# Values of the full layers by halves of the heads, and a last normalisation tile by tile: a four-layer attention kernel

## The chip, the cores and the metric

The kernel runs on one core of a Trainium2 chip. Its time is that of one execution on the device, in microseconds (us). TensorE is called PE here, VectorE DVE, ScalarE ACT, GpSimd POOL and SyncE SP; SP issues the DMAs.

## What is computed

Four layers on x of 2048 rows (the sequence) by 512 columns. Each is a layer norm, an attention of 32 heads of 16 and a residual. Layers 0 and 2 share weights and look back over a window of 256 positions ("sliding"); layers 1 and 3 share other weights and attend to everything, with no mask ("full").

```python
def _A_ref(x, wqkv, wo):          # _B_ref: the same without the mask
    B, S, D = x.shape
    H = 32; Dh = D // H; W = 256
    qkv = (x @ wqkv).reshape(B, S, 3, H, Dh).transpose(2, 0, 3, 1, 4)
    q, k, v = qkv[0], qkv[1], qkv[2]
    scores = jnp.einsum("bhqd,bhkd->bhqk", q, k) * (Dh ** -0.5)
    idx = jnp.arange(S)
    mask = (idx[:, None] - idx[None, :] >= 0) & (idx[:, None] - idx[None, :] < W)
    p = _softmax(jnp.where(mask[None, None], scores, -1e9), axis=-1)
    o = jnp.einsum("bhqk,bhkd->bhqd", p, v)
    return o.transpose(0, 2, 1, 3).reshape(B, S, D) @ wo

x = x + _A_ref(_layernorm(x), A_wqkv, A_wo)
x = x + _B_ref(_layernorm(x), B_wqkv, B_wo)
x = x + _A_ref(_layernorm(x), A_wqkv, A_wo)
x = x + _B_ref(_layernorm(x), B_wqkv, B_wo)
```

Everything is float32.

## The kernel before

**Units.** The sequence is cut into 4 chunks of 512 queries (c = 0 to 3) and 16 key tiles of 128; the heads into 8 quads (qd = 0 to 7). A float32 product of a projection is made of float16 high and low parts, three products for each of four slices of 128 inputs: 12 matmuls give one output tile of 128 by 512. That is a *piece* of side work, and four pieces are a *work*: the keys K(l,c), queries Q(l,c), values VV(l,c) or output projection OO(l,c) of layer l and chunk c, 48 matmuls each. In layer 3 keys, queries and output projection are cut further by pairs of quads (K3, Q3, O3).

**Attention.** `attention` (L897) walks through chunks and quads (in layer 3 through pairs t, then chunks, then quads). In a full layer a quad has 16 steps, one for each key tile. A step makes two score tiles (`exps`, L655; matmuls L663), ACT takes the exp of each, 128 by 1024 (L667), and 8 matmuls two steps later multiply them with the values (L707). A column of ones in the values (17 columns per head) yields the sum. Three score buffers hold what PE is ahead of ACT. In a sliding layer a quad has three steps with narrower tiles; POOL masks their edges (L729, L732), and the matmuls with the values are at L739. `epilogue` (L626) divides, splits the result into high and low parts (L645, L646), and four DMAs put it into the transposed output tile `oh`. In full layers the low part (L646) is made on POOL.

**Side work.** The order of PE's instructions is written out by the program; the other engines' order comes from the framework's scheduler. Between the steps of attention the class `Side` (L808) emits pieces of works. In sliding layers a chunk has 24 steps, and `step` emits up to a piece or so per step by a planner's clock (a matmul costs .222 on it). In full layers `share` (L869) deals out single groups of matmuls against a budget; there a 128-wide product is cut into four matmuls of 32 columns (L407 to L409) that together fill the one free bank, `acc[1]` (`bank`, L389). The next tile waits until DVE has copied this bank. When the steps of a `Side` are over, `finish` (L880) forces out in one run whatever is left. A work may start when its dependencies are done and one of two weight buffers (`weights`, L372) is free.

**Values.** `values` (L567) multiplies the transposed chunk with the value weights, tile by tile (i = 0 to 3), and copies each into `vt`. In full layers a chunk's `vt` has 4 tiles by 32 heads by 17, in 4 buffers (tag "vf"), and all four chunks are made before the full layer starts: as side work of the sliding layer, in its tail, and the last one (`lasts`) in the very end. Order of the lists: side0 (L1039), side2 (L1048), side1 (L1057), side3 (L1063); tails and lasts (L1075 to L1077).

**The end of a sliding layer** is not beside any attention. `wo` (L591) makes the last chunk's residual: for each of four row tiles 12 matmuls, DVE multiplies and adds (L601, L602), x is stored, and `stats` (L429) takes mean and variance. After the fourth tile `norm` (L431) runs one `rsqrt` (L39, 12 small DVE operations on a column per tile) and then, per tile, three operations (L439 to L442) that write the normalised tile as high and low parts `xh`. `transpose` (L456) then issues four transposing DMAs on SP, which fill the chunk's `xc`. The chunk's keys follow: 4 pieces, each with a maximum over squares (L515, L530), a high and a low part (`sp`, L490 to L493) and DMAs into `kf` in DRAM; then `key_shift` (L555) sets a row of `kf` from these maxima. Only then can `load_full` (L684) load the first keys `kt` of the full layer. Meanwhile PE makes the values of the last chunk.

**The kernel's end** is the last epilogue and `wo_part` (L609) of the last pair and chunk: four tiles of 3 matmuls, on DVE a multiplication (L621) and an addition (L622) each, and a store.

Of the kernel before, what the change touches and what calls it, by code (L numbers as in the profile page):

```python
# [38 lines left out]
def rsqrt(nc, vp, tag, var):  # L39

    v = vp.tile([P, 4], F32, name=f"v{tag}", tag="lnv")
    y = vp.tile([P, 4], F32, name=f"y{tag}", tag="lny")
    z = vp.tile([P, 4], F32, name=f"z{tag}", tag="lnz")
# [145 lines left out]
def fast_path(ctx, tc, flag, a_x, a_wqkv, a_wo, b_wqkv, b_wo, out):  # L189
# [182 lines left out]
    def weights(ty, s, n, t=None):  # L372

        w = wp.tile([P, NC, 2, D], F16, name=f"w{n}", tag="w", bufs=WB)
        if t is None:
            nc.sync.dma_start(w, wd[ty, s])
            return w
        nc.sync.dma_start(w[:, :, :, :P], wd[ty, s][:, :, :, t * P:(t + 1) * P])
        return w
# [18 lines left out]
    def mms(ps, pairs, after=1.6):  # L398
# [6 lines left out]
        for i, (a, b) in enumerate(pairs):  # L405
# [6 lines left out]
            spent(MM)  # L412
            if i < len(pairs) - 1:
                if PH["full"]:
                    yield MM
            else:
                PH["free"] = clock[0] + after
# [13 lines left out]
    def norm(l, c, xs):  # L431

        mv = ST.pop((l, c))[1]
        y = rsqrt(nc, vp, f"{l}_{c}", mv[:, :, 1])
        out = []
        for i in range(4):
            xn = vp.tile([P, D], F32, name=f"xn{l}_{c}_{i}", tag="xn", bufs=1)
            xh = vp.tile([P, 2, D], F16, name=f"xh{l}_{c}_{i}", tag="xh", bufs=XNB)
            norm1 = lambda o: nc.vector.tensor_scalar(o, xs[i], mv[:, i, 0:1], y[:, i:i + 1], op0=ALU.subtract, op1=ALU.mult)  # L439
# [15 lines left out]

    def transpose(l, c, xns):  # L456

        xc = XC[l, c] = wp.tile([P, 2, NC, QC], F16, name=f"xc{l}_{c}", tag="xc", bufs=NQ)
        for i in range(4):
            yield "wait", XNR[l, c] + 2.3 * i  # L460
            nc.sync.dma_start(xc[:, :, :, i * P:(i + 1) * P].rearrange("p b k n -> p (b k) n"),
                              xns[i].rearrange("p b n -> p (b n)"), transpose=True)

    def project(l, s, c, act, ht=None, first=None):
# [3 lines left out]
        if not first:  # L468
            w = weights(ty, s, n, ht)
# [97 lines left out]
    def values(l, c, act, first=None):  # L567
        n = f"{l}_{c}"
        if not first:
            w = weights(l % 2, 2, f"v{n}")  # L570
            yield wait(8)
            xc = XC[l, c]
        vt = V[l, c] = wp.tile([P, 4, H, DH + 1], F32, name=f"vt{n}",
                               tag="vf" if l % 2 else "vw", bufs=NQ if l % 2 else VB)
        nc.gpsimd.memset(vt[:, :, :, DH:], 1.0)
        for i in range(4):
            ps = bank()
# [5 lines left out]
            if first:  # L583
                nc.vector.tensor_tensor(vt[:, i, :, :DH], src, first[2].rearrange("p (h d) -> p h d", d=DH), ALU.mult)
            elif act:
                nc.scalar.activation(vt[:, i, :, :DH], src, AF.Copy)  # L586
            else:
                nc.vector.tensor_copy(vt[:, i, :, :DH], src)
            yield -MM if PH["full"] else -12 * MM

    def wo(l, c):  # L591
# [4 lines left out]
        for i in range(4):  # L596
# [8 lines left out]
            if i == 3:  # L605
# [3 lines left out]
    def wo_part(c, t):  # L609
# [6 lines left out]
        for i in range(4):  # L616
            ps = bank()
            yield from mms(ps, [(o[:, a, i * P:(i + 1) * P], w[:, b, :]) for a, b in TERMS])
            d = vp.tile([P, D], F32, name=f"dx3_{c}_{t}_{i}", tag="xn", bufs=1)
            k = 4 * c + i  # L620
            nc.vector.tensor_tensor(d, ps, gcol[1], ALU.mult)  # L621
            nc.vector.tensor_add(xs[i], xs[i], d)  # L622
# [3 lines left out]
    def epilogue(l, c, qd, a):  # L626
# [19 lines left out]
        (nc.gpsimd if l % 2 else nc.vector).tensor_tensor(hl[:, 1], o, hl[:, 0], ALU.subtract)  # L646
# [52 lines left out]
    def attn_full(l, c, qd, kt, qt, a):  # L699
        for j in range(NT):  # L700
# [4 lines left out]
            def pv(j=j, es_=es_):  # L705
                for h in range(4):
                    nc.tensor.matmul(a[32 * h:32 * h + DH + 1, :], V[l, j // 4][:, j % 4, 4 * qd + h, :],  # L707
# [189 lines left out]
    def attention(l, works):  # L897
# [5 lines left out]
        for t in range(NHT if l == 3 else 1):  # L903
            for c in range(NQ):
                qds = range(2 * t, 2 * t + 2) if l == 3 else range(NQD)
                if l == 1:

                    sd = sd or Side(NT * NQD * NQ, works[0], works[1])
# [6 lines left out]
                for qd in qds:  # L915
                    nxt = load(l, c, qd + 1) if qd + 1 in qds else None
# [19 lines left out]
    def T(l, c):  # L936
        return Work(later(lambda: transpose(l, c, XN.pop((l, c)))), 0.0, ("T", l, c), [("N", l, c)], aside=True)
# [188 lines left out]
```

## Time and profile before

| | us |
|---|---|
| median of 3 runs | 2864.93 (2863.16 to 2867.7) |
| the profiled execution | 2864.46 |
| its span | 2862.7 |
| layer 0, chunk 1 of the attention | about 170 to 310 |
| end of layer 0 (no attention) | about 517 to 580 |
| layer 1, exps | 580.7 to 1526.9 |
| layer 2, attention | 1536 to 1836 |
| end of layer 2 (no attention) | 1836 to 1896 |
| layer 3, exps | 1896.1 to 2838.5 |

Busy shares of the whole span: PE 93%, ACT 82%, DVE 37%, POOL 22%. The mean granted clock of PE is 0.979.

How to read the profile: times are us from the span's start. A row of the timeline has the start, the length from the first to the last end of a group of equal instructions that follow each other, engine, line and operation, the tile written and those read, the shape, and the count; in brackets the idle time of the engine just before and what ended it. Matmuls are pipelined, so a group's length includes the last one's drain. A row of windows has the length of a stretch and the time that each engine was busy in it. A row of waits has the us in total, the times and the longest one.

### The profile page before, as it was taken

The numbers are of one execution on the slowest core, as the hardware profiler recorded it, in microseconds if no ns is written. First come the engines' busy times: TensorE is split into PE (matmuls) and PEld (weight loads), VectorE is DVE, ScalarE is ACT, GpSimd is POOL, SyncE is SP. The second block draws the span as 40 slices with busy tenths as digits, with TensorE's granted clock in tenths as the row PEclk, the third lists the DMA queues.
The fourth block names the chain that finished last, engine by engine and source line by source line (L and its number), as shares of the span: only waits on it lengthen the run. The fifth ranks groups of instructions, "written<-read, shape, count | busy, mean of one in ns | idle before, by whom it ended". The sixth has DMA issues, their size and how long they took to land.

```text
span 2862.7 us, 58733 instructions
## 1 busy us (share of the span) xinstructions
PE 2668.1 (93%) x23298; PEld 766.6 (27%) x23298; DVE 1048.1 (37%) x2194; ACT 2352.5 (82%) x2643; POOL 627.5 (22%) x1183
## 2 busy tenths in 40 slices
PE   8777989799999999999999888999999999999997
PEld 4222433322222222222223333322222222222221
DVE  7667656411113212311224667722222322223222
ACT  3443656299999999999996666569999999999996
POOL 3547565101100000000003567500000000000000
PEclk9888999899999999999999999999999999999998
DMA  6857666522223222322343665542433333333331
GB/s 225 229 181 191 219 189 201 179 101 88 88 70 104 90 70 88 111 83 70 97 112 116 177 189 146 161 135 89 126 102 103 113 121 119 111 101 110 112 97 57
DMA packets 317423, 363.10 MB, mean 127 GB/s; under 512 B 120913, under 2 KB 223825, under 8 KB 309841
## 3 DMA queue, kind: packets, MB, share of 16 engines
q1 hardware_dynamic: 317136, 359.24, 41.5%
q8 instruction: 185, 3.03, 0.4%
q14 instruction: 102, 0.83, 0.1%
HBM read 229.64 MB, written 96.99 MB: 114 GB/s over the span
## 4 chain that ended last, share of the span: by engine, by line
PE 68%; ACT 10%; DVE 8%; issue 6%; DMA 3%; POOL 3%; SPq 1%; ACTq 0%; DVEq 0%; POOLq 0%
PE acc L707 28%; PE s L663 18%; ACT e L667 9%; PE b L411 9%; PE acc L408 8%; PE acc L739 3%; PE bs L411 2%; DVE ot L633 1%; DMA oh<-hl 1%; DVE xh L442 1%; SPq L650 1%; POOL w L338 1%; POOL e L732 1%; DVE xn L439 1%; DVE xh L439 1%
## 5 line engine op out<-in xcount | busy, mean ns | idle before, releaser
L667 ACT ACTIVATE e<-s 128x1024 f32<-128x1024 f32 (+2 forms) x2432 | 2235.3, 1199 | 115.1 <-PE s L663 108.1
L707 PE MATMUL acc<-e,vt 128*17 128x512 f32 x8192 | 1078.0, 598 | 3.7 <-DVE ot L633 1.5
L663 PE MATMUL s<-qt,kt 64*128 64x512 f16 (+3 forms) x5504 | 791.1, 355 | 70.8 <-ACT e L667 36.3
L663 PEld LDWEIGHTS <-kt 64*128 64x128 f16 x5504 | 222.6, 94 | 894.6 <-issue 851.3
L646 POOL TENSOR_TENSOR hl<-o,hl 128x512 f16<-128x512 f32 x64 | 74.2, 1159 | 999.8 <-DVE hl L645 923.3
L633 DVE STREAM_TRANSPOSE ot<-acc 128x512 f32<-128x512 f32 x128 | 91.2, 712 | 545.6 <-PE acc L707 448.0
L732 POOL TENSOR_SCALAR_AFFINE_SELECT e<-e 128x256 f32<-128x256 f32 x512 | 229.6, 456 | 160.1 <-ACT e L667 159.7
L739 PE MATMUL acc<-e,vt 128*17 128x384 f32 (+2 forms) x2816 | 213.4, 398 | 27.5 <-POOL e L729 26.6
L729 POOL TENSOR_SCALAR_AFFINE_SELECT e<-e 128x256 f32<-128x256 f32 x448 | 205.3, 464 | 113.7 <-ACT e L667 111.8
L707 PEld LDWEIGHTS acc<-e,vt 128*17 128x17 f32 x8192 | 136.3, 95 | 343.6 <-issue 314.5
L411 PE MATMUL b<-xc,w 128*128 128x512 f16 x636 | 154.6, 396 | 7.3 <-DMA xc<-xh 6.2
L492 DVE TENSOR_SCALAR sp<-acc,es 128x512 f16<-128x512 f32 x32 | 23.9, 748 | 323.6 <-PE acc L408 323.6
L490 ACT ACTIVATE sp<-b,es 128x512 f16<-128x512 f32 x53 | 36.4, 687 | 123.4 <-PE b L411 119.5
L498 POOL TENSOR_TENSOR sq_h<-sp_h 128x512 bf16<-128x512 f16 x27 | 29.1, 1077 | 451.5 <-DVE sp_h L492 451.5
L408 PE MATMUL acc<-xc,w 128*32 128x512 f16 x1536 | 127.2, 379 | 0.4 <-DVE sp L493 0.2
L498 POOL TENSOR_TENSOR sq<-sp 128x512 bf16<-128x512 f16 x32 | 33.3, 1039 | 405.3 <-DVE sp L492 405.3
L411 PE MATMUL b<-wv,xc 128*128 128x512 f16 x456 | 110.1, 395 | 11.0 <-DMA wv<-wd 11.0
L408 PE MATMUL acc<-xc,w_h 128*32 128x512 f16 x1296 | 114.5, 379 | 2.3 <-DVE km L530 2.3
L586 ACT ACTIVATE vt<-b 128x512 f32<-128x512 f32 x38 | 22.7, 597 | 102.7 <-PE b L411 102.7
L621 DVE TENSOR_TENSOR dx<-acc,gcol 128x512 f32<-128x512 f32 x60 | 41.5, 691 | 178.8 <-PE acc L408 178.8
L408 PE MATMUL acc<-wo,oh 128*32 128x512 f16 x1296 | 102.8, 379 | 0.7 <-DVE m L542 0.7
L411 PE MATMUL b<-wo,oh 128*128 128x512 f16 x390 | 91.5, 384 | 9.7 <-DMA oh<-hl 9.0
(164 smaller groups left out, 1728.0 us busy)
## 6 DMA issues: line engine op xcount, KB each, us to landing
kt<-kf SPq DMA_DIRECT2D x128, 512.0 KB
qt<-qs SPq DMA_DIRECT2D x128, 256.0 KB
xd<-x SPq DMA_DIRECT2D x96, 256.0 KB
x<-xd SPq DMA_DIRECT2D x96, 256.0 KB
w<-wd SPq DMA_DIRECT2D x22, 1024.0 KB
kt<-kw SPq DMA_DIRECT2D x64, 256.0 KB
oh<-hl SPq DMA_DIRECT2D x512, 32.0 KB
wv<-wd SPq DMA_DIRECT2D x15, 1024.0 KB
```

Of the source, the lines that this page charges most:

```text
L408: nc.tensor.matmul(ps[g:g + 32], a[:, g:g + 32], b, start=(i == 0), stop=(i == len(pairs) - 1), skip_group_check=True)
L411: nc.tensor.matmul(ps, a, b, start=(i == 0), stop=(i == len(pairs) - 1))
L439: norm1 = lambda o: nc.vector.tensor_scalar(o, xs[i], mv[:, i, 0:1], y[:, i:i + 1], op0=ALU.subtract, op1=ALU.mult)
L498: nc.gpsimd.tensor_tensor(sq, sp[:, 0], sp[:, 0], ALU.mult)
L633: nc.vector.transpose(ot.rearrange("p b r -> p (b r)"), a)
L646: (nc.gpsimd if l % 2 else nc.vector).tensor_tensor(hl[:, 1], o, hl[:, 0], ALU.subtract)
L663: nc.tensor.matmul(ps[:, h, s0:s0 + wd_], kt[R * h:R * h + R, pr, kc:kc + P], qt[R * h:R * h + R, pr, qc:qc + wd_], start=True, stop=True)
L667: nc.scalar.activation(e[:, :, w0:w1], ps[:, :, w0:w1], AF.Exp, scale=SCALE)
L707: nc.tensor.matmul(a[32 * h:32 * h + DH + 1, :], V[l, j // 4][:, j % 4, 4 * qd + h, :], es_[h // 2][:, h % 2, :], start=(j == 0), stop=(j ...
L729: nc.gpsimd.affine_select(v, v, pattern=[[0, 2], [-1, P]], compare_op=ALU.is_gt, fill=0.0, base=0, channel_multiplier=1)
L732: nc.gpsimd.affine_select(v, v, pattern=[[0, 2], [1, P]], compare_op=ALU.is_ge, fill=0.0, base=0, channel_multiplier=-1)
L739: nc.tensor.matmul(a[32 * h:32 * h + DH + 1, q * P:(q + nb) * P], V[l, (4 * c + j) // 4][:, j % 4, 4 * qd + h, :], es_[h // 2][:, h % 2, s ...
```

## The change

1. **Values by halves.** In full layers `vt` now holds 8 key tiles (two chunks) of one half of the heads, still 4 buffers. `values` takes the halves to make. A half product is 256 columns wide. Lower halves (quads 0 to 3) are made where the whole was made, ahead of the full layer. Most upper halves become side work of the full layer: in layer 1 those of chunks 0, 1 and 3, in a `Side` of their own over the first 64 steps (quads 0 to 3 of chunk 0); `side1` follows in a second one. In layer 3 the upper half of chunk 0 goes to (pair 0, chunk 0), of chunk 2 to (pair 0, chunk 2) and of chunk 3 to (pair 1, chunk 0). VV(1,2) and VV(3,1) stay whole, in the tails.
2. **The last chunk of a sliding layer tile by tile.** `wo` with `tail` set runs, after each tile's statistics, the `rsqrt` on that tile's one column, normalises the tile and issues its transposing DMA.
3. **Works that move.** K(1,0) from chunk 1 of layer 0 to chunk 2, K(1,1) from chunk 2 to 3; Q(1,1) from layer 1's side work to layer 0's tail, behind the last normalisation; the value works V(3,0) from chunk 2 of layer 2 to chunk 3 (lower half), and the tails start with a value work.
4. **The kernel's end.** The last epilogue's low part is made on DVE; in the last `wo_part` the additions of tiles 0 and 2 go to POOL, and `dx` uses other buffers (tag "oe").

```diff
-    def norm(l, c, xs):
+    def norm(l, c, xs, tiles=range(4)):
-        mv = ST.pop((l, c))[1]
-        y = rsqrt(nc, vp, f"{l}_{c}", mv[:, :, 1])
+        mv = ST[l, c][1]
+        i0, i1 = tiles[0], tiles[-1] + 1
+        y = rsqrt(nc, vp, f"{l}_{c}_{i0}", mv[:, i0:i1, 1])
...
+    def transposed(l, c, i, xh):
+        if (l, c) not in XC:
+            XC[l, c] = wp.tile([P, 2, NC, QC], F16, name=f"xc{l}_{c}", tag="xc", bufs=NQ)
+        nc.sync.dma_start(XC[l, c][:, :, :, i * P:(i + 1) * P].rearrange("p b k n -> p (b k) n"),
+                          xh.rearrange("p b n -> p (b n)"), transpose=True)
...
-    def values(l, c, act, first=None):
+    def values(l, c, act, first=None, halves=(0, 1)):
...
+        dst = {}
+        if l % 2:
+            for h in halves:
+                m = l, h, c // 2
+                if m not in V:
+                    V[m] = wp.tile([P, 8, HH, DH + 1], F32, name=f"vt{l}_{h}_{c // 2}", tag="vf", bufs=NQ)
+                    nc.gpsimd.memset(V[m][:, :, :, DH:], 1.0)
+                dst[h] = V[m][:, 4 * (c % 2):4 * (c % 2) + 4]
...
-                yield from mms(ps, [(xc[:, b, k, i * P:(i + 1) * P], w[:, k, a, :]) for k in range(NC) for a, b in TERMS])
+                yield from mms(ps, [(xc[:, b, k, i * P:(i + 1) * P], w[:, k, a, :D1 - D0]) for k in range(NC) for a, b in TERMS], us=us)
...
-            if i == 3:
+            if tail:
+                transposed(l + 1, c, i, norm(l + 1, c, xs, (i,))[0])
+            elif i == 3:
                 XN[l + 1, c] = norm(l + 1, c, xs)
...
-            d = vp.tile([P, D], F32, name=f"dx3_{c}_{t}_{i}", tag="xn", bufs=1)
+            last = (c, t) == (NQ - 1, NHT - 1)
+            d = vp.tile([P, D], F32, name=f"dx3_{c}_{t}_{i}", **(dict(tag="oe") if last else dict(tag="xn", bufs=1)))
-            nc.vector.tensor_add(xs[i], xs[i], d)
+            (nc.gpsimd if last and i % 2 == 0 else nc.vector).tensor_tensor(xs[i], xs[i], d, ALU.add)
...
-        (nc.gpsimd if l % 2 else nc.vector).tensor_tensor(hl[:, 1], o, hl[:, 0], ALU.subtract)
+        (nc.gpsimd if l % 2 and (l, c, qd) != (3, NQ - 1, NQD - 1) else nc.vector).tensor_tensor(hl[:, 1], o, hl[:, 0], ALU.subtract)
...
-                    sd = sd or Side(NT * NQD * NQ, works[0], works[1])
+                    sd = sd or Side(NT * NQD // 2, works[0], works[1])
...
+                    if (l, c, qd) == (1, 0, NQD // 2):
+                        sd.finish()
+                        sd = Side(NT * NQD * NQ - NT * NQD // 2, works[1], works[2])
...
-            return [..., PR(1, 2), T(1, 0), K(1, 0)]
+            return [..., PR(1, 2), T(1, 0)]
-            return [..., K(0, 3), OO(0, 1), Q(0, 3), PR(1, 3), VV(0, 3), T(1, 1), K(1, 1)]
+            return [..., K(0, 3), OO(0, 1), Q(0, 3), PR(1, 3), VV(0, 3), K(1, 0), T(1, 1)]
-        return [..., VV(1, 0), OO(0, 2), VV(1, 1), T(1, 2), K(1, 2), Q(1, 0)]
+        return [..., K(1, 1), OO(0, 2), VV(1, 0, True, (0,)), VV(1, 1, True, (0,)), T(1, 2), K(1, 2), Q(1, 0)]
...
-            return [OO(2, 1), VV(2, 3), VV(3, 0), T(3, 1), K3(1, 0, True)]
-        return [OO(2, 2), T(3, 2), K3(2, 0, True)]
+            return [OO(2, 1), VV(2, 3), T(3, 1), K3(1, 0, True)]
+        return [OO(2, 2), VV(3, 0, True, (0,)), T(3, 2), K3(2, 0, True)]
...
+        v = {(0, 0): 0, (0, 2): 2, (1, 0): 3}.get((t, c))
+        if v is not None:
+            a.append(upper(3, v))
...
-    tails = {0: [OO(0, 3), VV(1, 2), T(1, 3), K(1, 3)],
-             2: [OO(2, 3), VV(3, 1), VV(3, 2), Q3(0, 0, True), T(3, 3), K3(3, 0, True)]}
-    lasts = {0: [VV(1, 3)], 2: [VV(3, 3)]}
+    tails = {0: [VV(1, 2), OO(0, 3, True), Q(1, 1, True, [("N", 1, 3)]), T(1, 3), K(1, 3)],
+             2: [VV(3, 1), OO(2, 3, True), VV(3, 2, True, (0,)), Q3(0, 0, True, [("N", 3, 3)]), T(3, 3), K3(3, 0, True)]}
+    lasts = {0: [VV(1, 3, True, (0,))], 2: [VV(3, 3, True, (0,))]}
```

More of the change, by code (lines that the diff above doesn't have):

```diff
@@ L947, in K3, with Q3 @@
         return Work(later(keys, 3, c, act, ht), PK / 4, ("K3", c, ht), [("T", 3, c)], True)
-    def Q3(c, ht, act=False):
-        return Work(later(queries, 3, c, act, ht), PK / 4, ("Q3", c, ht), [("T", 3, c)], True)
+    def Q3(c, ht, act=False, after=()):
+        return Work(later(queries, 3, c, act, ht), PK / 4, ("Q3", c, ht), [("T", 3, c), *after], True)
     def shift3(ht):
@@ L959, in O3, with VV, OO @@
         return Work(wo_part(c, ht), PO / 4, None, [("O", 3, c, ht)], True)
[L961 to L965 removed]
+    def VV(l, c, act=True, halves=(0, 1)):
+        return Work(later(values, l, c, act, None, halves), PV * len(halves) / 2, ("V", l, c, halves), [("T", l, c), ("P", l % 2, 2)], True)
+    def OO(l, c, tail=False):
+        return Work(later(wo, l, c, tail), PO, ("N", l + 1, c), [("O", l, c, NHT - 1), ("P", l % 2, 3)], True)
     def NN(c, after=()):
```

91 lines of the change are left out of this document (45 added, 46 removed).

## Prediction

> **What bounds the kernel now.** I began with the page: its span line and its engine line.
>
> ```profile
> span 2862.7 us, 58733 instructions
> PE 2668.1 (93%) x23298; PEld 766.6 (27%) x23298; DVE 1048.1 (37%) x2194; ACT 2352.5 (82%) x2643; POOL 627.5 (22%) x1183
> ```
>
> Those shares average stages with different limits, so next come windows cut by stage: chunk 1 of layer 0, then the two full layers. The columns are length, PE, PEld, DVE, ACT and POOL busy, the PE clock, the DMA share and GB/s.
>
> ```profile
> 170.00:310.00 140.00, 106.91 (x832) 42.34 (x833) 101.60 (x186) 62.99 (x79) 79.82 (x153) 0.87 0.71 207
> ...
> 581.00:1526.00 945.00, 933.36 (x8736) 221.11 (x8736) 203.12 (x452) 943.39 (x1024) 70.18 (x66) 1.00 0.29 88
> ...
> 1896.00:2839.00 943.00, 926.44 (x8185) 219.95 (x8183) 231.29 (x455) 939.62 (x1025) 64.69 (x58) 1.00 0.34 105
> ```
>
> The full layers are ACT's: 943.39 of 945 us and 939.62 of 943 us of exps. Work that PE does there beside the exps is free until it makes ACT wait. In layer 0 ACT is idle more than half the time and PE has 140 − 106.9 = 33 us of idle: PE and what it waits for set the end. The third view is PE's waits in that chunk (us in total, times, longest):
>
> ```profile
> PE acc L739 <- POOL e L729: 8.5, 4, 3.4
> PE b L515 <- DVE sp L493: 8.4, 1, 8.4
> PE b L411 <- DMA wv<-wd: 8.2, 1, 8.2
> ```
>
> So 25 of those 33 us are a few lumps, waits of an in-order PE for one instruction elsewhere. Last I read the timeline at the ends of the sliding layers, where a chain PE, DVE, DMA, PE, DMA sets the time and neither ACT nor PE is full.
>
> The profiled execution took 2864.46 us, of which the span is 2862.7; the median of the runs shown is 2864.93. I sum against the first and add the 0.47 between them at the end.
>
> **Side pieces in the sliding layers.** A piece is 12 matmuls of 512 columns. In layer 2 three piece starts give the price:
>
> ```profile
> 1743.33 2.76 PE L411 MATMUL b<-wo,oh 128*128 128x512 f16 x12
> ...
> 1747.56 2.76 PE L411 MATMUL b<-wv,xc 128*128 128x512 f16 x12
> ...
> 1754.15 2.76 PE L411 MATMUL b<-wv,xc 128*128 128x512 f16 x12
> ```
>
> The first two are 4.23 us apart, one attention step with its piece; the next 6.59, which is such a step and one of 2.36 without a piece. A piece therefore costs 1.87. Its 12 matmuls take 12 × .216 = 2.59 (2.76 less the last one's drain of .38, over 11). The step around them is 1.64, so a half piece, 12 × .108 = 1.30, gives a step of 2.94: .58 more than none.
>
> - Layer 0, chunk 1 loses K(1,0), 4 pieces: **−7.5**. Bounds: 0, if the lumps grow into the space, and −12, if 4 × 2.76 go whole with a little waiting.
> - Chunk 2 gives K(1,1) away and takes K(1,0): 0. Chunk 3 takes 4 pieces and halves 8: 4 × 2.59 − 8 × 1.30 = 0 in matmuls, 4 × 1.87 − 8 × 1.29 = −2.8 in steps. I take **−1**, and keep both ends.
> - Layer 2: chunk 2 loses V(3,0), 4 × 1.87 = −7.5; chunk 3 takes its lower half, +2.3. **−5.2**, bounds −7 to −1.
>
> ACT's and DVE's copies of these tiles cost nothing: chunk 1's window has DVE busy 101.6 and ACT 63.0 of 140. If that cover were gone, each would cost its copy, some .6.
>
> **The end of layer 0.** The rows of the timeline, in order:
>
> ```profile
> 531.94 0.69 DVE L601 TENSOR_TENSOR dx<-bs,gcol 128x512 f32<-128x512 f32 x1 [7.92 <-PE bs L411]
> ...
> 534.12 0.18 DVE L429 BATCH_NORM_AGGREGATE mv<-st 128x2 f32<-128x6 f32 x1
> ...
> 542.10 0.17 DVE L44 TENSOR_SCALAR v<-mv 128x4 f32<-128x4 f32 x1
> ...
> 544.49 0.55 DVE L439 TENSOR_SCALAR xn<-x,mv,y 128x512 f32<-128x512 f32 x1
> ...
> 550.44 0.69 DVE L442 TENSOR_TENSOR xh<-xn,xh 128x512 f16<-128x512 f32 x1
> ...
> 555.10 4.62 PE L411 MATMUL bs<-xc,w 128*128 128x512 f16 x12 [15.43 <-DMA xc<-xh]
> ...
> 560.13 0.69 DVE L530 TENSOR_REDUCE km<-b 128x1 f32<-128x512 f32 x1 [9.00 <-PE b L515]
> ...
> 560.74 0.74 DVE L493 SCALAR_TENSOR_TENSOR sp<-bs,es,sp 128x512 f16<-128x512 f32 x1
> ...
> 569.68 2.76 PE L411 MATMUL bs<-wv,xc 128*128 128x512 f16 x12
> ...
> 574.36 1.60 SPq L684 DMA_DIRECT2D kt<-kf  x3
> ...
> 580.14 0.61 PE L663 MATMUL s<-qt,kt 64*128 64x512 f16 x4
> ```
>
> Before, DVE normalises from 531.94 to 551.13, 19.2 us, with one rsqrt chain (542.10 to 544.49 = 2.39) for all four tiles. K(1,3), the work that needs all four transposes, starts 3.97 later. The change runs that chain once a tile. Its operands shrink from four columns to one, but a .17 op on four columns is already all fixed cost, so I give it the same 2.39. A tile is then 2.18 (dx to aggregate) + .18 + 2.39 + 6.64/4 = 6.41, four are 25.6; in DVE's order Q(1,1) puts four sp ops of .74 and one reduction of .69 between them, 3.7. Together 29.3: **the last tile is ready 10.1 later**, at 561.2, and K(1,3) starts at 565.2. Four transposes at once take longer than one; that is why 3.97 may be 3, and a chain on one column may be 1.8: K start's bounds are 561 to 566.
>
> The transposes of tiles 0 to 2 are earlier, but K(1,3) multiplies all 512 columns. On SP the load of V(1,3)'s half weights stands ahead of the last transpose, and waits for Q(1,1)'s last matmul. PE has Q(1,1) behind the output projection, whose last tile leaves it near 540; 10.4 us of matmuls end well ahead of 561, so that wait hides. If Q's sp buffers hold PE up, it doesn't, and the queue of kf and kt loads behind it is late by as much.
>
> From K's start to the first scores: before 580.14 − 555.10 = 25.0, ended by V(1,3) (from 569.68, 4 pieces, 10.4). After, that path is 14.6 + 5.2 = 19.8. What is late next is kt: its loads were issued at 574.36, 19.3 after K's start. In the DMA view from 574 to 582, in slices of .2 us, they fill
>
> ```profile
> DMA  9300001318895358999999999999997300009018
> ```
>
> from 575 to 580.4; the first of three I put at 578, 22.9 after K's start, less up to 1.5 since the weights load in front of them is half. I take 22.0. First scores at 587.2: **+7.1** (bounds +3 to +9).
>
> **The end of layer 2** has the same edit with only one sp op and one reduction of Q3(0,0) between:
>
> ```profile
> 1854.20 0.69 DVE L601 TENSOR_TENSOR dx<-bs,gcol 128x512 f32<-128x512 f32 x1 [4.78 <-PE bs L411]
> ...
> 1872.71 0.69 DVE L442 TENSOR_TENSOR xh<-xn,xh 128x512 f16<-128x512 f32 x1
> ...
> 1878.91 4.37 PE L411 MATMUL bs<-xc,w_h 128*128 128x512 f16 x12 [3.71 <-DMA xc<-xh]
> ...
> 1885.03 2.76 PE L411 MATMUL b<-wv,xc 128*128 128x512 f16 x12
> ...
> 1889.40 1.39 SPq L684 DMA_DIRECT2D kt<-kf  x3
> ...
> 1895.49 0.60 PE L663 MATMUL s<-qt,kt 64*128 64x512 f16 x4
> ```
>
> 25.6 + 1.4 = 27.0 on DVE in place of 19.2; K3 at 1854.20 + 27.0 + 3.97 = 1885.2, and not 1878.91. The half V path from there is 6.1 + 5.2 = 11.3; kt's is 10.5 to its issue and 3.7 more, 14.2. Scores at 1899.4: **+3.9** (bounds +1 to +6).
>
> **Six upper halves as side work** of the full layers: 6 × 4 × 12 groups of .108 = 31 us of PE time, less Q(1,1)'s 10.4. ACT covers it as long as it is spread: by the windows all side work of today leaves ACT 1.6 and 3.4 us short of full. I take 0, bound +4. But `finish` forces out in one run what is left when its steps are over. The program built from the change issues such runs of 37 groups in layer 3 at the end of (pair 0, chunk 2) and (pair 1, chunk 0). What a run does to the exps, layer 1's end shows:
>
> ```profile
> 580.74 10.19 ACT L667 ACTIVATE e<-s 128x1024 f32<-128x1024 f32 x11
> ...
> 1505.85 1.05 PE L707 MATMUL acc<-e,vt 128*17 128x512 f32 x8
> ...
> 1527.65 2.77 PE L408 MATMUL acc<-wv,xc 128*32 128x512 f16 x48 [0.79 <-DVE vt L588]
> ...
> 1531.22 2.77 PE L408 MATMUL acc<-wv,xc 128*32 128x512 f16 x48 [0.79 <-DVE vt L588]
> ...
> 1536.08 1.51 ACT L667 ACTIVATE e<-s 128x768 f32<-128x768 f32 x2 [9.24 <-PE s L663]
> ```
>
> There ACT stands 9.24 us. A tile repeats after 3.57: 2.77 and .80 until DVE has copied the one bank. Twelve groups of 256 columns at half of (2.77 − .38)/11 = .217 take 1.30, with a drain of .16 and a wait of .52: 1.98. A run of 37, one group and three tiles, is .79 + 2 × 1.98 + 1.30 = 6.05. Ahead of the next scores stand 8 P·V matmuls, .87 (1.05 less the last one's drain), and the scores themselves, some .4 of the .61 above; three score buffers hold 3 exps of .93 = 2.8. Stall 6.05 + .87 + .4 − 2.8 = 4.5 a run: **+9.0** for two (bounds 0, if PE was far ahead, to 14, by scaling the 9.24 for 112 groups with less reserve). Layer 1's own end has 16 matmuls more, 4 groups: **+.9**.
>
> The price of half-width groups is not shown: no row of these quarters is narrower than 512, so the other price is a rival below. [...]
>
> **The kernel's end:**
>
> ```profile
> 2842.92 1.15 POOL L646 TENSOR_TENSOR hl<-o,hl 128x512 f16<-128x512 f32 x1 [26.91 <-DVE hl L645]
> ...
> 2849.60 0.69 DVE L621 TENSOR_TENSOR dx<-b,gcol 128x512 f32<-128x512 f32 x1 [6.81 <-PE b L411]
> ```
>
> The low part on DVE takes .69 in place of 1.15 and starts .1 earlier, −.56. Two of eight DVE ops of .7 go to POOL, −1.25. **−1.8** (bounds 0 to −2).
>
> Sum: −7.5 − 1 − 5.2 + 7.1 + 3.9 + 9.0 + .9 − 1.8 = **+5.4**: 2869.9, and on the median 2870.3.
>
> **Rivals.**
>
> 1. *The forced runs hide* (0 in place of 9.0): 2861.3. For it: PE's side work is a queue that can run ahead. Against: the 9.24 at layer 1's end.
> 2. *Layer 0's chunk 1 sheds its lumps; the kernel is faster.* With K(1,0) gone, K(0,2)'s squares and the weights' transposes each get one attention step more ahead of them in PE's order; a wait of 8.4 behind a step of 4.2 halves. It decides from 11 us recovered beyond my 7.5, of the 25 in lumps; at 16 the time is 2854. Against: the 8.2 wait for the weights' load is not moved by it, and POOL's masks stay.
> 3. *Half-width groups are not half price.* The nearest row:
>
> ```profile
> 511.15 0.61 PE L663 MATMUL s<-qt,kt 64*128 64x256 f16 x8
> ```
>
> Eight of 256 columns start within .54, 67 ns each, two beside each other. Four quarters so paced take .27: a tile 3.3 to 3.9 as a run, each forced run 6 us longer, 2882.3. Against: 512-wide quarters at 57.7 ns.
> 4. *The tile-by-tile normalising is not what delays K*, because PE comes late anyway (Q(1,1) and V(1,2) in front): as my forecast within 3 us.
>
> **How the numbers follow.** 0.2% is 5.7 us, about what a measurement of this kernel can tell from no change. Forecast, with rival 4: .45, 2864 to 2877 (.02 faster, .18 same, .25 slower). Rival 1: .14 (.05, .09). Rival 2: .22 (.20, .02). Rival 3: .12, all slower. The rest, a wait I don't see: .07 (.01, .01, .05). Faster .28, same .30, slower .42. The range 2853 to 2884 leaves out the lower part of rival 2, the upper of rival 3 and most of the rest, some .18.
>
> **What would show it.** In the changed kernel: DVE's last xh of each tail about 10 and 8 us later than here, counted from the first dx, and the first full-layer scores 7 and 4 later; two holes of some 4 us in ACT in layer 3 (none: rival 1; 10: rival 3); chunk 1 of layer 0 near 132 us (under 122: rival 2). The forecast is wrong if a one-column chain is much below 2.39, or if the first kt load comes early.

## The result, and the profile after

The changed kernel took 2884.01 us (median of 4 runs, 2880.85 to 2885.37), the kernel before on the same chip 2864.62: a ratio of 1.0066, 95% interval 1.0054 to 1.0078. It is 19 us slower. The forecast was 2870.3, slower by 5; the time lies at the upper end of the range, 2884. So the direction was right and the size wrong by a factor of more than three, and the work is to find which terms of the sum were off.

From the page of the changed kernel, its span and its engines:

```profile
span 2882.7 us, 60872 instructions
PE 2672.4 (93%) x24306; PEld 794.9 (28%) x24306; DVE 1051.4 (36%) x2285; ACT 2356.4 (82%) x2659; POOL 625.2 (22%) x1180
```

The shares are those of before: a change that costs 20 us of span (2862.7 to 2882.7) hardly shows in them. The stages show it. The table cuts both spans at the first exp of each chunk or layer (ACT's L667, after the change L687), with the ends of the sliding layers from the last exp to the first exp of the full layer:

| stage | before | after | change | forecast |
|---|---|---|---|---|
| up to the first exp | 65.7 | 67.0 | +1.3 | 0 |
| layer 0, chunk 0 | 105.0 | 104.1 | −0.8 | 0 |
| layer 0, chunk 1 | 139.3 | 125.2 | −14.1 | −7.5 |
| layer 0, chunk 2 | 110.2 | 115.6 | +5.4 | 0 |
| layer 0, chunk 3 | 95.9 | 99.3 | +3.4 | −1 |
| end of layer 0 | 64.6 | 73.4 | +8.8 | +7.1 |
| layer 1 | 955.3 | 958.8 | +3.5 | +0.9 |
| layer 2, attention | 298.7 | 288.1 | −10.6 | −5.2 |
| end of layer 2 | 61.3 | 72.4 | +11.0 | +3.9 |
| layer 3 | 942.4 | 957.0 | +14.6 | +9.0 |
| kernel's end | 24.2 | 21.9 | −2.4 | −1.8 |
| sum | | | +20.0 | +5.4 |

Changes are taken before rounding. The first 1.3 us are scatter: over the kernels shown here the first exp comes at 65.7 to 67.6.

First the end of layer 0, in the timeline of the changed kernel. The rows are: the first dx, the first operation of a one-column rsqrt chain and its last, the last xh, the keys K(1,3), kt's loads, the first scores.

```profile
527.03 0.69 DVE L618 TENSOR_TENSOR dx<-bs,gcol 128x512 f32<-128x512 f32 x1 [7.70 <-PE bs L409]
...
529.43 0.15 DVE L42 TENSOR_SCALAR v<-mv 128x1 f32<-128x1 f32 x1
...
531.54 0.16 DVE L48 SCALAR_TENSOR_TENSOR y<-z,y 128x1 f32<-128x1 f32 x1
...
556.38 0.69 DVE L441 TENSOR_TENSOR xh<-xn,xh 128x512 f16<-128x512 f32 x1
...
560.78 5.17 PE L409 MATMUL b<-xc,w 128*128 128x512 f16 x12 [9.97 <-DMA xc<-xh]
...
580.10 1.41 SPq L704 DMA_DIRECT2D kt<-kf  x3
...
584.14 0.82 PE L683 MATMUL s<-qt,kt 64*128 64x512 f16 x6 [2.82 <-DMA kt<-kf]
```

A chain on one column takes 529.43 to 531.74, 2.3 us, against 2.39 on four: nearly all of it is fixed cost. The last xh is ready 30.0 us after the first dx (19.2 before) and the keys start 33.75 after it (23.2 before). The scores wait for kt, no longer for V(1,3). All of that was in the forecast, but for the scores, which come 23.4 after the keys' start and not 22.0.

The same place in layer 2. The rows are: the last piece of chunk 3's keys K3(2,0), the first dx, the last xh, the keys K3(3,0), then mk's store, a weights load and kt's loads on SP, and the first scores:

```profile
1834.61 4.44 PE L409 MATMUL b<-xc,w_h 128*128 128x512 f16 x12 [2.34 <-DMA xc<-xh]
...
1854.65 0.69 DVE L618 TENSOR_TENSOR dx<-b,gcol 128x512 f32<-128x512 f32 x1 [5.60 <-PE b L409]
...
1880.94 0.69 DVE L441 TENSOR_TENSOR xh<-xn,xh 128x512 f16<-128x512 f32 x1
...
1885.36 5.08 PE L409 MATMUL b<-xc,w_h 128*128 128x512 f16 x12 [13.81 <-DMA xc<-xh]
...
1894.59 0.36 SPq L567 DMA_DIRECT2D kf<-mk  x1
...
1897.63 0.54 SPq L376 DMA_DIRECT2D w_h<-wd  x1
1898.27 1.63 SPq L704 DMA_DIRECT2D kt<-kf  x3
...
1903.14 1.03 PE L683 MATMUL s<-qt,kt 64*128 64x512 f16 x4 [5.55 <-DMA kt<-kf]
```

The chain on DVE took 27.0 as forecast, but the first scores come 17.8 after the keys' start, not 14.2. And the first dx is 23.2 after layer 2's last exp (1831.5), where it was 19.4. So 3.7 of the 11.0 arose ahead of the first dx. The first row above shows where: the last piece of K3(2,0) had to wait for its transposes and then ran slowly. Before, in the timeline of the kernel before, it did neither:

```profile
1835.41 2.76 PE L411 MATMUL b<-xc,w_h 128*128 128x512 f16 x12
```

That was .65 after the last exp; now it is 3.1, and the granted clock is .62 during this piece, 1.00 before. The later start is there in every kernel below that has V(3,0)'s half in chunk 3 (2.5 to 3.5 after the last exp), and not in e4, which hasn't; so it belongs to the side work that moved. The slow piece, 1.7 us, isn't in all of them: in e7, e10 and e11 it takes 2.75, and the first dx comes 20.5 to 21.4 after the last exp.

In layer 3, the end of the first pair's chunk 2, ACT and PE:

```profile
2076.89 4.88 ACT L687 ACTIVATE e<-s 128x1024 f32<-128x1024 f32 x5
...
2079.68 1.05 PE L727 MATMUL acc<-e,vt 128*17 128x512 f32 x8
...
2080.55 0.29 PE L406 MATMUL acc<-wv,xc 128*32 128x256 f16 x4
...
2081.36 1.49 PE L406 MATMUL acc<-wv,xc 128*32 128x256 f16 x48 [0.52 <-DVE vt L605]
...
2083.38 1.50 PE L406 MATMUL acc<-wv,xc 128*32 128x256 f16 x48 [0.52 <-DVE vt L605]
...
2085.40 1.49 PE L406 MATMUL acc<-wv,xc 128*32 128x256 f16 x48 [0.53 <-DVE vt L605]
2086.83 0.60 PE L683 MATMUL s<-qt,kt 64*128 64x512 f16 x4
...
2087.32 5.63 ACT L687 ACTIVATE e<-s 128x1024 f32<-128x1024 f32 x6 [5.55 <-PE s L683]
```

The forced run is there: from 2080.55 to 2086.83, 6.28 us (forecast 6.05), and ACT stands for 5.55 (forecast 4.5). A second such hole of 5.55 follows at the end of (pair 1, chunk 0). The two are 11.1 of layer 3's 14.6; the other 3.5 lie in quads with denser side work, for example the first two with 29.7 and 30.5 us where they took 28.9 and 29.3.

Last, PE's waits in layer 0 (us in total, times, longest), first in chunk 1, then in chunk 2:

```profile
PE b L518 <- DVE sp L496: 6.4, 1, 6.4
...
PE b L409 <- DMA wv<-wd: 1.1, 1, 1.1
```

```profile
PE b L409 <- DMA wo<-wd: 7.0, 1, 7.0
```

Chunk 1 lost most of the 8.2 us lump of the weights' load, which the prediction had said would stay; chunk 2, whose longest wait was 3.6, got one of 7.0 on the load of OO(0,1)'s weights.

### The profile page after: what moved, and what is told of

Read it like the earlier page. It is cut to its first block, busy times and chain, and to the rows that moved or that the text cites. A ratio compares the mean times of both kernels' runs of the same rounds, so it can differ in the third digit from the quotient of the medians.

```text
span 2882.7 us, 60872 instructions
## 1 busy us (share of the span) xinstructions
PE 2672.4 (93%) x24306; PEld 794.9 (28%) x24306; DVE 1051.4 (36%) x2285; ACT 2356.4 (82%) x2659; POOL 625.2 (22%) x1180
## 4 chain that ended last, share of the span: by engine, by line
PE 66%; ACT 10%; DVE 9%; issue 7%; DMA 4%; POOL 3%; SPq 1%; ACTq 0%; DVEq 0%; POOLq 0%
PE acc L727 27%; PE s L683 17%; ACT e L687 10%; PE acc L406 9%; PE b L409 9%; PE acc L759 2%; PE bs L409 1%; DVE ot L653 1%; DVE xh L441 1%; DVE xn L438 1%; DVE xh L438 1%; POOL wr L331 1%; POOL w L336 1%; POOL e L752 1%; POOL e L749 1%
## 5 line engine op out<-in xcount | busy, mean ns | idle before, releaser
L687 ACT ACTIVATE e<-s 128x1024 f32<-128x1024 f32 (+2 forms) x2432 | 2237.8, 1181 | 171.9 <-PE s L683 166.2
L409 PE MATMUL b<-xc,w 128*128 128x512 f16 x672 | 163.8, 397 | 16.3 <-DMA xc<-xh 15.2
L406 PE MATMUL acc<-xc,w 128*32 128x512 f16 x1344 | 109.9, 379 | 0.2 <-DVE sp L496 0.2
L409 PEld LDWEIGHTS <-w 128*128 128x128 f16 x720 | 69.2, 102 | 123.0 <-issue 50.1
L605 DVE COPY vt<-acc 128x256 f32<-128x256 f32 (+1 forms) x36 | 18.4, 512 | 230.5 <-PE acc L406 230.5
L495 DVE TENSOR_SCALAR sp_h<-acc,es 128x512 f16<-128x512 f32 x27 | 20.0, 741 | 217.0 <-PE acc L406 216.9
```

Source lines behind the costliest of these rows:

```text
L406: nc.tensor.matmul(ps[g:g + 32], a[:, g:g + 32], b, start=(i == 0), stop=(i == len(pairs) - 1), skip_group_check=True)
L409: nc.tensor.matmul(ps, a, b, start=(i == 0), stop=(i == len(pairs) - 1))
L687: nc.scalar.activation(e[:, :, w0:w1], ps[:, :, w0:w1], AF.Exp, scale=SCALE)
```

## The experiments

The theory from these views: the slowdown is the rsqrt chains on DVE in both tails (some 11 us) and the two forced runs (11 us), with halves and moves paying back less than they seem to. Rivals: the tails are slow for their new order on PE, or narrow groups are dear. All ratios are to the kernel before on the same chip; the changed kernel's is 1.0066.

### e1: normalise once, after four tiles

```diff
-    tails = {0: [VV(1, 2), OO(0, 3, True), Q(1, 1, True, [("N", 1, 3)]), ...
-             2: [VV(3, 1), OO(2, 3, True), ...
+    tails = {0: [VV(1, 2), OO(0, 3), Q(1, 1, True, [("N", 1, 3)]), ...
+             2: [VV(3, 1), OO(2, 3), ...
```

> The changed kernel with one edit undone: in the last chunk of a sliding layer the rsqrt chain and the normalisation run once, after the fourth tile, and the four transposes follow. Everything else (halves, works moved, order of the tails) stays. Theory (the four chains on DVE delay the keys): three chains of 2.33 us leave each tail, so the keys K(1,3) start 7 us sooner after the first dx and K3(3,0) some 5 us; the first scores of both full layers follow, and the time falls from 2884 by 10 to 13 to about 2872. Rival (the keys wait for PE, which has V(1,2) and Q(1,1) in front of them now): the time stays within 3 us of 2884.

2871.6 us, 1.0028 (1.0019 to 1.0038): the tile-by-tile part costs some 11 us. But the two tails share it unlike the forecast: layer 2's end shrinks from 72.4 to 66.4, layer 0's only from 73.4 to 70.1. The timeline of e1 shows why (first dx, Q(1,1)'s last product, last xh, the last of Q(1,1)'s stores, V(1,3)'s weights, the last two transposes, the keys):

```profile
524.85 0.69 DVE L618 TENSOR_TENSOR dx<-bs,gcol 128x512 f32<-128x512 f32 x1 [7.43 <-PE bs L409]
...
540.63 2.75 PE L409 MATMUL bs<-xc,w 128*128 128x512 f16 x12
...
545.97 0.69 DVE L441 TENSOR_TENSOR xh<-xn,xh 128x512 f16<-128x512 f32 x1
...
546.46 0.72 SPq L509 DMA_DIRECT2D qs<-sp  x1
547.28 0.61 SPq L376 DMA_DIRECT2D wv<-wd  x1
547.94 4.82 SPq L459 DMA_TRANSPOSE xc<-xh  x2
...
554.71 5.30 PE L409 MATMUL b<-xc,w 128*128 128x512 f16 x12 [11.33 <-DMA xc<-xh]
```

The third xh was ready at 544.8, its transpose is issued at 547.94: from 544.47 on SP issues four of Q(1,1)'s stores, whose last `sp` tile is ready on DVE at 545.5. V(1,3)'s weights come behind them and add only their own .66: Q(1,1)'s last product, for which this load waits by the prediction, had ended at 543.4. The keys start 8 us after the last xh, not 4.

### e2: no forced runs in layer 3

An upper half that isn't done is carried into the next (pair, chunk), with a little more side work per step:

```diff
-                if l != 1 or c == NQ - 1:
+                if l == 3 and t < 2 and (t, c) != (1, NQ - 1):
+                    while any(not w.carry for w in sd.q):
+                        sd.one(True)
+                    left = sd.q
+                elif l != 1 or c == NQ - 1:
                     sd.finish()
...
-            self.lag = max(self.lag - 0.29, -0.3)
+            self.lag = max(self.lag - (0.29 if not any(w.carry for w in self.q) else 0.36), -0.3)
```

> The changed kernel, but an upper half that is not done at the end of its (pair, chunk) in layer 3 goes on in the next one, a little denser while there is one (.36 us of side work a step in place of .29); the runs of 37 groups at two boundaries are gone, the longest run left is 12 groups. Nothing else changes. Theory (ACT's two holes of 5.6 us come from the forced runs): layer 3 shrinks by 10 to 11 us, 2884 to about 2873.5. Rival (narrow groups are dear wherever they run, so their PE time shows up elsewhere): 2880 or above.

2876.04 us, 1.0047 (1.0033 to 1.0061); layer 3 took 950.2 in place of 957.0. The holes of 5.55 are gone, and 6.8 us with them, not 10 to 11. What is now forced out at two boundaries is output projection, six groups in two parts with a wait for DVE between them. It still stops ACT, as e2's timeline shows at one of them:

```profile
2262.76 0.83 PE L406 MATMUL acc<-wo,oh 128*32 128x512 f16 x12 [0.79 <-DVE dx L641]
...
2264.02 4.71 ACT L687 ACTIVATE e<-s 128x1024 f32<-128x1024 f32 x5 [1.39 <-PE s L683]
```

Two of these are 2.8; the rest of the missing 4 us is spread over quads with denser side work (the three worst take 31.2 us, these holes included, most others 29.3). Neither theory had it right: the runs cost what the profile showed, and spreading the work isn't free. Narrow groups as such are not dear: 48 of their matmuls, 12 groups, take 1.49.

### e3: both

> Both edits together: normalisation once after four tiles, and no forced runs in layer 3. If the two costs lie one behind the other on the path, the gains add: 2884 - 11.5 - 10.5 = 2862, 2.6 us below the kernel before. If what hides behind one is uncovered by the other (kt's loads, PE's products in the tails), the sum is smaller: 2866 to 2870.

2869.42 us, 1.0017 (1.0007 to 1.0027). The gains of e1 and e2 are .0038 and .0019 of ratio, together .0057; e3 gained .0049, within the intervals of the sum. They add, as far as these intervals can tell. But e3 is still 6 us above before, where halves and moves alone were to put it below: the tails take 69.2 and 67.2 us (64.6 and 61.3 before), layer 3 951.1 (942.4 before).

### e4: the tile-by-tile part on the kernel before

> The kernel before with the tile-by-tile normalisation of the last chunk of the sliding layers and nothing else. Theory: 6.4 us later keys in each tail (four tiles of 6.4 on DVE in place of 19.2), less 1.5 in the second, where four transposes in a row took longer; 2864.6 + 11 to 13 = about 2876.5. Rival (tile by tile is harmless by itself, transposes come earlier and only the rearranged tails cost): 2862 to 2866.

Of the diff this takes only `norm`, `transposed`, `wo` and the two `OO(..., True)`. 2879.51 us, 1.0055 (1.0041 to 1.0068), 16 us slower. In its profile the ends of the sliding layers take 70.9 and 68.9 us, 6.3 and 7.6 more than before: the mechanism alone. In the first tail that is the 6.4 expected to a tenth of a us; in the second 4.9 was expected. There the last xh came 7.9 later and not 6.4, with operations of Q3(0,0) on DVE between the tiles, and the transposes gave back .5 and not 1.5. The remaining 2 us of the 16 lie within the interval.

### e5: Q(1,1) back into layer 1

e1 with Q(1,1) taken out of the tail and one list for layer 1:

```diff
-    tails = {0: [VV(1, 2), OO(0, 3), Q(1, 1, True, [("N", 1, 3)]), T(1, 3), K(1, 3)],
+    tails = {0: [VV(1, 2), OO(0, 3), T(1, 3), K(1, 3)],
...
-        a = [Q(1, c, False) for c in (2, 3)]
+        a = [Q(1, c, False) for c in (1, 2, 3)]
```

> The kernel of e1 (changed kernel, normalisation once after four tiles) with Q(1,1) back from layer 0's tail into layer 1's side work; layer 1 has one list of side works for all its 512 steps again, .33 us a step in place of .29, so that the run at its end stays as long as before the change. In e1 the last xh of layer 0's tail is ready 21.8 us after the first dx, but the keys start 8 us later, where 4 us were enough before. Theory (SP: the last two transposes stand behind Q(1,1)'s four pairs of stores and behind V(1,3)'s weights, which wait for Q(1,1)'s last product): with Q(1,1) gone the keys start 23 to 24 us after the first dx in place of 29.9, and the time falls by 5 to 6.5 us, 2871.6 to about 2866. Rival (the transposes themselves are slow, or DVE is): keys 27 us or more after the first dx, 2869 to 2872, or above if layer 1 pays for Q(1,1).

The timeline of e5 answers for SP's queue (first dx, last xh, the last two transposes, the keys):

```profile
529.68 0.69 DVE L618 TENSOR_TENSOR dx<-bs,gcol 128x512 f32<-128x512 f32 x1 [7.28 <-PE bs L409]
...
548.18 0.69 DVE L441 TENSOR_TENSOR xh<-xn,xh 128x512 f16<-128x512 f32 x1
548.21 2.61 SPq L459 DMA_TRANSPOSE xc<-xh  x2
...
553.16 5.28 PE L409 MATMUL bs<-xc,w 128*128 128x512 f16 x12 [15.75 <-DMA xc<-xh]
```

The keys start 23.5 us after the first dx, as before the change, and the end of layer 0 takes 64.7 us (70.1 in e1, 64.6 before). Q(1,1) in the tail cost 5.3 there: of the 6.4 by which the keys come sooner, 2.6 are DVE's (the last xh 19.2 after the first dx, 21.8 in e1) and 3.8 lie between the last xh and the keys, where SP's queue was. As a whole the kernel took 2872.29 us, 1.0019 (1.0008 to 1.0030): against e1 no difference that these intervals can tell. Layer 1 took 2.5 longer, with Q(1,1), one list and .33 a step, and other stages of the profiled execution, the slowest of nine, were longer too. So it is shown that Q(1,1) in the tail delays the keys, and the stores and the weights load weren't tried apart; the expected 5 us of the total aren't shown. V(1,3)'s half brings nothing here: 64.7 with it, 64.6 with the whole.

### e6: the weights load ahead of kt

```diff
-            all_of(lasts[l], works[l + 1][0])
+            all_of(lasts[l], () if l else works[l + 1][0])
```

> The kernel of e1, but nothing of layer 3 is prefetched beside the last values of layer 2. In e1 SP issues a weights load at 1886.11, as V(3,3)'s last product frees its buffer, and kt's loads right behind it at 1886.74, 3.9 us after mk's store; before the change that was 1.9. Theory (kt stands in SP's queue behind a load that waits for PE): kt is issued about 2 us after mk's store, the first scores of layer 3 come some 1.8 us sooner after K3's start, 15.3 in place of 17.1. Rival (kt waits for mk's store to land): 3.9 and 17.1 as in e1. The whole moves by too little to be timed; later weights may cost layer 3 a run at (pair 0, chunk 0).

Inconclusive: the edit didn't change the order. The load was still issued ahead of kt's, at 1888.89 and 1889.52. The one run gave 2878.14 and settles nothing.

### e9: one chain for two tiles

```diff
-            if tail:
-                transposed(l + 1, c, i, norm(l + 1, c, xs, (i,))[0])
+            if tail and i % 2:
+                for u, xh in zip((i - 1, i), norm(l + 1, c, xs, (i - 1, i))):
+                    transposed(l + 1, c, u, xh)
+            elif tail:
+                pass
```

> The changed kernel with one rsqrt chain for every two tiles of the tails in place of one for every tile; the transposes of a pair follow it. Two chains of 2.33 us fewer in each tail. Theory (DVE's chains are what delays the keys): the last xh some 4.7 us sooner after the first dx in both tails (22.3 in the second in place of 27.0), the time 2882 - 9 = 2873; somewhat less if SP's queue then holds the transposes of the first tail, as it did in e1. Rival (it is the transposes one by one that cost): the time stays at 2880 or above.

2872.62 us, 1.0036 (1.0022 to 1.0049). In layer 2's tail (e9's timeline: first dx, last xh, keys)

```profile
1844.53 0.69 DVE L618 TENSOR_TENSOR dx<-b,gcol 128x512 f32<-128x512 f32 x1 [5.78 <-PE b L409]
...
1865.87 0.67 DVE L441 TENSOR_TENSOR xh<-xn,xh 128x512 f16<-128x512 f32 x1
...
1870.85 4.45 PE L409 MATMUL b<-xc,w_h 128*128 128x512 f16 x12 [10.44 <-DMA xc<-xh]
```

the last xh is ready 22.0 after the first dx, 22.3 expected. The dose fits: two chains fewer, 5.0 us sooner, 9 us of time. The number of chains sets when the last xh is ready, not the transposes one by one. In the first tail the order of SP's queue counts as well: e9's end of layer 0 takes 67.5, less than e1's 70.1 although it has a chain more, because its keys start 5 us after the last xh and e1's 8.

### e7 and e8: keep what paid

e7 is the changed kernel with halves for V(1,0), V(1,1) and V(3,0) only, and with one list of side works in layer 1 again; e8 adds denser side work to layer 1 (.33 in place of .29 a step).

```diff
-    tails = {0: [VV(1, 2), OO(0, 3, True), Q(1, 1, True, [("N", 1, 3)]), T(1, 3), K(1, 3)],
-             2: [VV(3, 1), OO(2, 3, True), VV(3, 2, True, (0,)), ...]}
-    lasts = {0: [VV(1, 3, True, (0,))], 2: [VV(3, 3, True, (0,))]}
+    tails = {0: [OO(0, 3), VV(1, 2), T(1, 3), K(1, 3)],
+             2: [OO(2, 3), VV(3, 1), VV(3, 2), Q3(0, 0, True), T(3, 3), K3(3, 0, True)]}
+    lasts = {0: [VV(1, 3)], 2: [VV(3, 3)]}
...
-        v = {(0, 0): 0, (0, 2): 2, (1, 0): 3}.get((t, c))
+        v = {(0, 0): 0}.get((t, c))
...
-    works = [[side0(c) for c in range(NQ)], [[upper(1, c) for c in (0, 1, 3)], side1()], ...
+    works = [[side0(c) for c in range(NQ)], [[upper(1, c) for c in (0, 1)] + side1()], ...
```

> The changed kernel with those parts kept that paid in the traces so far: halves for V(1,0), V(1,1) and V(3,0) alone, whose upper halves are layer 1's first side work and side work of layer 3's (pair 0, chunk 0), so that no run is forced in layer 3; K(1,0) and K(1,1) a chunk later; the new end of the kernel. Normalisation once after four tiles, Q(1,1) in layer 1's side work, V(1,2), V(1,3), V(3,1), V(3,2), V(3,3) whole, and the tails' order as before the change. Theory: layer 0's chunks keep their 4 us, layer 2 its 7 us (11, less 3.5 given back at its end), the kernel's end 2; the tails and layer 3 go back to what they were; layer 1 pays up to 2. 2863 - 11 = 2852. Rival (half works gain nothing without the rearranged tails, or the gain in chunk 1 is given back in chunks 2 and 3): 2860 or above.

2853.69 us, 0.9962 (0.9949 to 0.9976): 11 us faster than before, as worked out from the stages.

> e7 with .33 us of side work a step in layer 1 in place of .29. The run that finish forces out at the end of layer 1 shrinks from 7.1 to 3.1 us of products. If ACT's hole at that end (10 us) is that run, the time falls by 3 to 4 us against e7, to about 2848; if denser steps slow the exps by as much, it stays.

2848.87 us, 0.9943 (0.9929 to 0.9956): the fastest median of all these kernels. ACT's first row behind layer 1's end, in e7 and then in e8:

```profile
1535.49 1.51 ACT L687 ACTIVATE e<-s 128x768 f32<-128x768 f32 x2 [10.03 <-PE s L683]
```

```profile
1531.04 1.51 ACT L687 ACTIVATE e<-s 128x768 f32<-128x768 f32 x2 [5.24 <-PE s L683]
```

The hole falls by 4.8, from 10.03 to 5.24, as the forced run falls from 7.1 to 3.1 us of products and loses one wait of .79 for DVE. The medians fall by 4.8 as well, though the two intervals overlap a little. This part owes nothing to the change: the run was there before.

In layer 2's end of e8 V(3,3) is whole, and PE frees its weights later:

```profile
1875.54 0.30 SPq L567 DMA_DIRECT2D kf<-mk  x1
...
1877.84 1.39 SPq L704 DMA_DIRECT2D kt<-kf  x3
...
1884.35 0.53 SPq L376 DMA_DIRECT2D w_h<-wd  x1
```

Here kt's loads go 2.3 us after mk's store, with the weights load behind them; in the changed kernel it was 3.7, with the load ahead. That speaks for SP's queue. In e4 too the load stands behind, and there it is 2.9, of which SP waits 2.1 for mk's store to land. Before, it was 1.9. From these gaps I estimate that the load ahead costs .8 to 1.8; it wasn't tried by itself.

### e10 and e11: what layer 0's part is worth

e10 is e8 with the keys at their old place; e11 is e8 with layer 0 as before the change.

```diff
-            return [..., PR(1, 2), T(1, 0)]
+            return [..., PR(1, 2), T(1, 0), K(1, 0)]
...
-            return [..., VV(0, 3), K(1, 0), T(1, 1)]
+            return [..., VV(0, 3), T(1, 1), K(1, 1)]
-        return [..., K(1, 1), OO(0, 2), VV(1, 0, True, (0,)), VV(1, 1, True, (0,)), ...]
+        return [..., VV(1, 0, True, (0,)), OO(0, 2), VV(1, 1, True, (0,)), ...]
```

> e8 with K(1,0) back in layer 0's chunk 1 and K(1,1) back in chunk 2; chunk 3 has V(1,0) and V(1,1) as halves still, and so only 12 pieces and 8 halves. By the price of a piece (1.87) the move itself is worth nothing: chunk 1 gets 7.5 us longer, chunk 3 7.5 shorter, the time stays within 3 us of 2849. Rival (chunk 1 was shortened by 14 because its lumps went, and chunk 2 got 5.5 and chunk 3 3.5 longer because others came): chunk 1 is 139 us again, chunk 2 110, chunk 3 about 86, and the three together tell whether the move gained anything.

2854.0 us, 0.9967 (0.9955 to 0.9980). Windows of layer 0's chunks 1, 2 and 3 in e10 (length, then busy PE, PEld, DVE, ACT, POOL, clock, DMA share, GB/s), and PE's longest wait in its chunk 3:

```profile
172.80:312.30 139.50, 105.81 (x826) 41.93 (x825) 100.88 (x185) 63.02 (x78) 78.87 (x151) 0.87 0.71 206
312.30:419.50 107.20, 97.61 (x834) 39.48 (x835) 66.17 (x134) 62.41 (x77) 67.39 (x144) 0.97 0.67 204
420.00:516.10 96.10, 84.22 (x834) 38.95 (x836) 53.88 (x121) 57.85 (x72) 51.87 (x129) 0.96 0.72 205
```

```profile
PE b L409 <- DMA xc<-xh: 6.3, 1, 6.3
```

This refutes the price of a piece that the prediction used. Chunk 3 lost eight half products, PE's busy time fell to 84.2 (93.5 before), and the chunk takes 96.1 us as before (95.9): the time came back, 6.3 us of it as a wait for K(1,2)'s transposes. And chunk 1 is 139.5 again, 126.2 in e8: with four pieces in it, 13 us, not 7.5. The three chunks together take 343.3, against 341.0 in e8, so the move of the keys is worth 2 us in these profiles. The whole is 5 us longer than e8, more than the 3 expected, but here too the intervals overlap a little.

> e8 with layer 0 as it was before the change: V(1,0) and V(1,1) whole in chunk 3, K(1,0) and K(1,1) at their old places, no upper halves in layer 1. What is left of the change is V(3,0) by halves and the new end of the kernel (and the denser side work of layer 1 from e8). Theory: layer 0's halves and moves are worth 4 us, layer 1's side work for them 1: 2849 + 3 = 2852. Rival (layer 0's part pays nothing in the end): 2846 to 2849.

2849.53 us, 0.9951 (0.9937 to 0.9965): no different from e8. In the profiles the three chunks take 4.5 us more in e11 (345.5 against 341.0), and layer 1, without the two upper halves, 2.6 less (950.3 against 952.8). Layer 0's halves and moves are worth nothing that these runs can tell; the time is nearer to the rival's 2846 to 2849 than to the theory's 2852, but the interval holds both. What pays of the change, by the stages of e11's profile against those before, is V(3,0) by halves (layer 2 with its end is 9.0 shorter) and the new end of the kernel (22.4, against 24.2 before and 23.4 in e4, which has the old end); neither was run alone. Layer 1 is 5.1 shorter by the denser side work, which isn't part of the change.

## Why the prediction was right in direction and too small

The stages missed by 28 us upwards and by 13.5 downwards. That these partly cancel, and that the time still came out at the end of the range, is luck and no merit of the sum.

- **The tails' DVE chain: right.** "Four are 25.6" and 27.0, 29.3 with what lies between; 27.0 and 30.0 were measured, e4 shows the cost alone and e9 the dose. Rival 4 (PE late anyway) is out.
- **The end of layer 2: mis-sized, +3.9 forecast, +11.0 measured.** Two steps failed. The sum began at the first dx and took for granted that it keeps its distance from the last exp; it came 3.7 later, since the last piece of chunk 3's keys, behind the side work that moved, waited and ran at a clock of .62. And "kt's is 10.5 to its issue and 3.7 more, 14.2" was 12.9 and 4.9, 17.8: a weights load that waited for PE stood in front of kt on SP (3.7 from mk's store to kt, 1.9 before), and PE, idle for 13.8 us, did its first 12 products in 5.1 us, at a granted clock of .53, where 4.4 (at .61) had been taken over from before. Why kt's 3.7 became 4.9 stays open.
- **The forced runs: right in place and length, too small in effect.** The term that failed is "three score buffers hold 3 exps", 2.8. When PE began the P·V matmuls ahead of the run (2079.68), behind the last scores, ACT had 2.1 us of exps left, to 2081.77. The sum with its terms as measured is the hole: 6.28 for the run, .87 for P·V (2079.68 to 2080.55), .5 from the next scores to their exp, less 2.1, is 5.55. The upper bound of 14 scaled "112 groups"; the rows at layer 1's end show 112 matmuls, which are 28 groups. Rival 1 is out, and so is rival 3: a half-width group costs (1.49 − .16)/12 = .11, half of a whole one.
- **A piece at 1.87 wherever it is: failed.** Chunk 1 of layer 0 gave 14.1 in place of 7.5, chunk 2 took 5.4 in place of 0 and chunk 3 3.4 in place of −1. The waits that end last there are few and long, and they move with the pieces: the weights' load left chunk 1 and one of 7.0 came in chunk 2; e10 took eight half products out of chunk 3 and got 6.3 us of wait. Rival 2 saw half of it: chunk 1 did shed a lump, 6.6 us beyond the forecast and not the 11 that rival 2 needed, and the other chunks took it up. In layer 2, whose rows the price came from, chunk 2 gave 11.3 for V(3,0)'s four pieces (83.0 to 71.7), 2.8 each, more than the 2.59 of their matmuls.
- **Layer 2's attention: more than forecast**, −10.6 in place of −5.2, of which 3.7 came back at its end; −6.9 is the part that counts.
- **SP's queue in layer 0's tail:** the prediction saw V(1,3)'s weights ahead of the last transpose and found that the wait hides behind DVE. In the changed kernel it does. With DVE made faster (e1) SP's queue did hold the last transposes, by Q(1,1)'s stores in front of them and hardly by the weights load.
- **Layer 1** cost 3.5 in place of .9. ACT stands 10.0 at its end (9.24 before), .8 more where .9 was forecast. Another 1.9 is one hole at 1448.86: PE had waited 1.63 for DVE there and then worked at a granted clock of .51 (1446.32 to 1448.86). The rest is denser quads; what the second list of side works has in that wasn't tried alone.

Rival 3 went by 67 ns a matmul, from a row of other matmuls 256 columns wide. In the changed kernel 48 half-width quarters in 1.49 us (row 2081.36) are 31 ns each, the last one's drain included, where 48 whole ones in 2.77 (row 1527.65 of before) are 57.7.

## What to carry to other kernels

To pipeline a short chain tile by tile multiplies its fixed cost (here 2.3 us a chain on one column, 2.39 on four): count the small operations, not their elements, and ask whether the consumer can start on one tile at all. Work moved out of a stage that is paced by a few long waits must be followed to the stage that takes it (here chunk 1 gave 14.1 us, and chunks 2 and 3 took back 8.8), up to the first instruction behind its end, and the queue of DMA issues checked for a store or a load that waits for another engine ahead of the one on the path (here 3.8 us between e1 and e5). How much a forced run of side work costs depends on how far the other engine is ahead at that moment: read it from the rows just before, not from the number of buffers (here 2.1 us of exps were left, where three buffers had been taken for 2.8).

## What the runs showed of the hardware

In the chain at 529.43 of the changed kernel an rsqrt operation on one column of 128 partitions takes .15 to .16 us, in the chain at 542.10 of the kernel before, on four columns, .16 to .17: the width makes next to no difference there. In the changed kernel PE's 12 matmuls of 512 columns took 5.17 us (from 560.78) and 5.08 (from 1885.36) right after 10.0 and 13.8 us without work, at granted clocks of .52 and .53, and 2.75 in a row with others (from 548.05), at 1.00. The loss doesn't grow with the pause in these rows: in the kernel before they took 4.37 after 3.7 us (from 1878.91, clock .61) and 4.62 after 15.4 (from 555.10, clock .58).
